# The old state set down by ScalarE, and small work moved to GpSimd, in an RWKV-7 and top-k expert kernel

## The chip, the cores and the metric

The kernel runs on one core of one Trainium2 chip. A core has TensorE (PE, matrix products), VectorE (DVE), ScalarE (ACT), GpSimd (POOL) and SyncE (SP, which here only issues transfers). The metric is the device time of one execution in microseconds, the median of several runs.

## The reference, cut to what matters

Two blocks follow each other. The first is a recurrence over 768 time steps for 4 batches of 8 heads, each with a state of 40 x 40:

```python
for t in range(S):
    y[:, :, t] = einsum('bhd,bhde->bhe', r_t, state)
    Sa = einsum('bhde,bhe->bhd', state, a_t)
    state = state * w_t[:, :, None, :] - einsum('bhd,bhe->bhde', Sa, b_t) + einsum('bhd,bhe->bhde', v_t, k_t)
```

The second takes the 3072 rows of `y` (320 wide) to one of 8 experts each. Of those that chose an expert, only the 80 with the largest gate weights are computed; all other rows are zero:

```python
expert_idx = argmax(x @ w_gate)
for e in range(E):
    tok_idx = the (at most) 80 rows of expert e with the largest gate_w
    out[tok_idx] = gate_w[tok_idx, None] * (maximum(x[tok_idx] @ w1[e], 0) @ w2[e])
```

## The kernel before, in words

**Units.** The recurrence is cut into chunks of 64 time steps; a unit is one chunk of a pair of batches (z) with all eight heads, so there are 24 units, and consecutive units belong to different pairs: a state written by unit n is read by unit n + 2. The heads stand in four pairs (g); the two heads of a pair (q) take the upper and lower 64 partitions. Within a chunk the decays are made cumulative (`pt` forwards, `qt` backwards, two DVE scans), the inputs are scaled with them, and the recurrence becomes products and the inversion of a unit-triangular matrix.

**Stages of a unit.** Seven units ahead, the preparation: `decays` (transpose w), `forward`, `backward`, `turned_a` and `decayed_a` (a, transposed, times `pt`), `doubled` (`qt` written twice side by side), `inverted` (transpose `qd`, multiply k and b: `scaled`), `operand`, `system` and `system_kept` (the matrix `nt`, sent to memory). Then the unit itself: `of_v`, `right` (adds the state times a), `diagonal`, `below`, `diagonal`, `beside`; `reads_g` transposes the state. One iteration later its output: `of_state`, `kept_state`, `turned`, `lower`, `summed`, then `logits`, and after one more iteration `logits_summed`.

**The output tile.** `y` is one PSUM tile (`ps_y` has one buffer), with 64 columns for outputs and 40 for the new state per head pair. `kept_state` puts the old state on those 40 columns by a product with the identity, four products a unit. `summed` adds the unit's contribution, then DVE multiplies the 40 columns by the last decay into `state` (line 522, one instruction for each q) and the other columns into `xT` (line 526). Until both are done, TensorE can't begin `of_state` of the next unit (line 416).

**The state.** It is kept with the two heads of a pair side by side, each on its own 64 partitions and zero on the other's, so that `right` can use it as the second operand of a product over 128 partitions.

**The inversion.** It is done on DVE for four units at a time, in 30 steps of two instructions (lines 381 and 384). `fetch` reads `nt` back from memory as `lt`, `begin` makes the start `tt` from it on GpSimd, `end` sends the solution to memory and reads it back as `dt`, which `diagonal` uses. In every group of four iterations, the first (n divisible by 4) fetches and begins, and the three others hold the steps: `pause(steps, us)` issues steps until their assumed cost is used up.

**Order.** Each engine works through its own queue in order, and `do` fixes that order as written in the loop over n: what stands earlier in the loop stands earlier in every engine's queue. A wait of one instruction holds all that is behind it on that engine. SyncE's queue of transfers is also in order.

**Selection and experts.** After the units, lists of the largest gate weights are merged, row numbers found by products with one-hot matrices, and the experts computed: `gather` (an indirect transfer by GpSimd), `tokens` (transpose), `first_half`, `second_half`, and an indirect transfer to the output. `keep_at_work` gives TensorE 40 products on a tile without meaning while the first rows are gathered. The small transfer `held` stands in SyncE's queue ahead of the weights of experts 3 to 7 and waits for the row numbers.

Of the kernel before, what the change touches and what calls it, by code (L numbers as in the profile page):

```python
# [8 lines left out]
F32 = mybir.dt.float32  # L9
BF16 = mybir.dt.bfloat16  # L10
I32 = mybir.dt.int32
AX = mybir.AxisListType.X
# [6 lines left out]
def kernel(  # L19
# [43 lines left out]
    NCI = NM // NG  # L63
    HB = 64
    assert N == B * S and DM == H * D and D <= HB and H % 2 == 0 and S % (2 * T) == 0 and BP == 2
    assert G * ZT == 512 and NG * 32 == 128 and E == 8 and 1 <= cap <= 128
    rounds = -(-cap // 8)
    capr = rounds * 8
    NF = DM // 128
# [60 lines left out]
    assert NL // NG >= 2 and capr <= 128 and NG * ZT <= MERGE + NG * capr  # L130


    ones_b = const.tile([128, 128], BF16, name="ones_b")
    behind_b = const.tile([128, 128], BF16, name="behind_b")
    seg_t = const.tile([128, E, 2 * NM], F32, name="seg")
    seg = seg_t.rearrange("p e m -> p (e m)")
    iot = const.tile([128, 1, cap], F32, name="iot")


    still = const.tile([128, 256], BF16, name="still")  # L140
    nc.vector.memset(still, 0.0)

    def keep_at_work(pool, tag, times, x=still):
        p = pool.tile([128, 256], F32, name="still_p", tag=tag)
        for _ in range(times):
            nc.tensor.matmul(p, lhsT=x[:, 0:128], rhs=x, start=True, stop=True)

    nc.gpsimd.tensor_copy(ones_b, ones)
    nc.gpsimd.tensor_tensor(out=behind_b, in0=strict, in1=ones, op=Alu.subtract)
    nc.gpsimd.memset(seg_t, 1.0)  # L150
    nc.gpsimd.memset(seg_t[:, :, 0:1], 0.0)
    iot_i = const.tile([128, cap], I32, name="iot_i")
    nc.gpsimd.iota(iot_i, pattern=[[1, cap]], base=1, channel_multiplier=0)
    nc.gpsimd.tensor_copy(iot[:, 0, :], iot_i)


    with ExitStack() as p1:
# [14 lines left out]
        def filled(name, n, shape, fill=0.0, where=lambda t: t):  # L172

            ts = [hold.tile(shape, F32, name=f"{name}{i}") for i in range(n)]
            for t in ts:
                engines[0].memset(where(t), fill)
                engines.reverse()
            return ts
# [13 lines left out]
        side = hold.tile([128, 1 + SLOTS, Z, H, HB], F32, name="side")  # L192
        nc.gpsimd.memset(side[:, 1:], 0.0)


        state = filled("state", BP, [128, Z * G * 2 * D + HB - D])
        og_t = filled("og", 2, [128, NG, 32])

        units = [(c, bp) for c in range(NC) for bp in range(BP)]
# [27 lines left out]
            return side[:, 1 + n % SLOTS]  # L227

        def own(n):
            return state[units[n][1]][:, 0 : Z * G * 2 * D].rearrange("p (z g q d) -> p z g q d", z=Z, g=G, q=2)  # L230

        def pairs(t):
            return t.rearrange("p (g q) d -> p g (q d)", q=2)
# [82 lines left out]

        def doubled(n):
            of[n]["qd"] = qd = sb.tile([128, G, Z, 2, T], F32, name="qd", tag="qd")
            nc.scalar.copy(qd.rearrange("p g z i t -> p (g z) i t"),  # L319
                           of[n].pop("qt")[:, :, :, 1:].rearrange("p g z t -> p (g z) t").unsqueeze(2)  # L320
                           .to_broadcast([128, G * Z, 2, T]))

# [105 lines left out]
        def kept_state(n):  # L428

            if n + BP < NU:  # L430
                for z in range(Z):
                    for q, m in enumerate(pars):
                        nc.tensor.matmul(of[n]["y"][m, z, :, T : T + D], lhsT=ident[m, m], rhs=own(n)[m, z, :, q, :],
                                         start=False, stop=False, skip_group_check=True)

        def right(n):
            o, sb_, pr = of[n], own(n), of[n]["pr"]
            for g in range(G):
                for z in range(Z):
                    nc.tensor.matmul(pr[halves[1 - z], 2 * g : 2 * g + 2, :], lhsT=o["ahT"][:, g, halves[z]],  # L440
                                     rhs=sb_[:, z, g, :, :], start=False, stop=False, skip_group_check=True)

        def right_kept(n):
            o = of[n]
# [25 lines left out]
                nc.scalar.copy(vu_of(n)[m, 1 - i, :, 0:D], of[n]["pr"][m])  # L470

        def reads_g(n):
            st = state[units[n][1]]
            p = ps_t.tile([128, Z, G, HB], F32, name="gp_", tag="t")
            for z in range(Z):
                for g in range(G):
                    for q, m in enumerate(pars):
                        at = ((z * G + g) * 2 + q) * D
                        nc.tensor.matmul(p[m, z, g, :], lhsT=st[m, at : at + HB], rhs=ident[m, m], start=z == 0 and g == 0,
                                         stop=True, skip_group_check=True)  # L480
            of[n]["gT"] = gT = sb.tile([128, Z, G, HB], F32, name="gT", tag="gT")
            nc.scalar.copy(gT, p)
# [25 lines left out]
        def summed(n):  # L508
            o = of[n]
            last = n + BP >= NU  # L510
            for z in range(Z):
                for g in range(G):
                    for q, m in enumerate(pars):
                        x = side[:, 0, z, 2 * g + q, :]
                        if not last:

                            x = bass.AP(x.tensor, x.offset, [x.ap[0], [(1 + n % SLOTS) * Z * H * HB, 2], [1, HB]])
                        nc.tensor.matmul(o["y"][m, z, g, 0 : T if last else T + HB], lhsT=o["s"][:, z, 2 * g + q, :], rhs=x,  # L518
                                         start=False, stop=True, skip_group_check=True)
            if not last:  # L520
                for q, m in enumerate(pars):
                    nc.vector.tensor_tensor(  # L522
                        out=own(n)[m, :, :, q, :], in0=o["y"][m, :, :, T : T + D],
                        in1=o["pt"][m, :, :, T : T + 1].rearrange("p g z o -> p z g o").to_broadcast([HB, Z, G, D]), op=Alu.mult)
            o["xT"] = xT = sb.tile([128, G, ZT], F32, name="xT", tag="xT")
            nc.vector.tensor_tensor(out=by_batch(xT).rearrange("p g z t -> p z g t"), in0=o["y"][:, :, :, 0:T],
                                    in1=o["pt"][:, :, :, 0:T].rearrange("p g z t -> p z g t"), op=Alu.mult)
            load(n + 3, "v")
# [20 lines left out]

        def logits_summed(n):  # L550
            i = share_of[n]
            nc.vector.tensor_reduce(logit[i][:, n - shares[i][0], :], of[n]["xb"][:, :, 2 * D :].rearrange("p g e -> p e g"),  # L552
                                    axis=AX, op=Alu.add)
            of[n].clear()

        def eight(src, dst, i, first=None):
# [110 lines left out]
        def do(f, *args):  # L667
            traced = nc.cur_bb.bb.instructions
            at = len(traced)
            f(*args)  # L670
            traced = nc.cur_bb.bb.instructions
            for i in traced[at:]:
                if i.engine in kinds:
                    if i.engine in latest:
                        tc.add_manual_dep(i, latest[i.engine], mybir.DependencyInfo(
                            mybir.DependencyClass.NoSync, mybir.DependencyReason.DATA), reason="order")
                    latest[i.engine] = i.name
# [4 lines left out]
        def pause(todo, us_):  # L682
            while todo and us_ > 0:
                cost, f = todo.pop(0)
                do(f)
                us_ -= cost
# [55 lines left out]
        for n in range(NU + 2):  # L742
# [29 lines left out]
                do(doubled, m + 1)  # L772
            if now:
                do(right_kept, n)
            if next_:
                do(turned_a, m + 1)
                do(decayed_a, m + 1)
            pause(small, 1)
            pause(steps, 0.7)
            if past:  # L780
                do(lower, o)
            if n == NU - 1:
# [13 lines left out]
            if not coming:  # L796
                pause(steps, 9 if n % NG == 1 else 5.5 if n % NG == 2 else 100)
                pause(rounds_, LISTS.get(n, 0))
            elif n % NG == 0:
                do(begin, m // NG)  # L800
            else:
                pause(steps, 6.7 if n % NG < NG - 1 else 100)
            if o >= 1:
                do(logits, o - 1)
            if turn:
# [25 lines left out]

    pieces = const.tile([128, NM, NP, E], BF16, name="pieces")
    rest = const.tile([128, NM, E], F32, name="rest")
    for x, last, first_piece in ((ids, 1, 0), (gates, 4, 2)):
        for i in range(first_piece, last):
            nc.gpsimd.tensor_copy(pieces[:, :, i, :], x)
            nc.gpsimd.tensor_tensor(out=rest if i + 1 < last else pieces[:, :, last, :], in0=x, in1=pieces[:, :, i, :], op=Alu.subtract)
            x = rest  # L840

    fw = ctx.enter_context(tc.tile_pool(name="fw", bufs=1))

# [19 lines left out]
    with ExitStack() as p2:  # L863
# [36 lines left out]
        for m0 in range(0, NM, CH):  # L900
# [3 lines left out]
            for m in range(m0, m0 + CH):  # L904
# [2 lines left out]
        late = const.tile([128, 256], BF16, name="late")  # L907
        nc.gpsimd.affine_select(out=late, in_=hot.rearrange("p m s -> p (m s)")[:, 0:256], compare_op=Alu.is_gt,
                                fill=0.0, base=-2, pattern=[[0, 256]], channel_multiplier=0)
        keep_at_work(ps_l, "still", 40, late)  # L910
        low = sl.tile([cap, NP * E], F32, name="low")
        nc.scalar.copy(low, ip)
        piece = [low[:, i * E : (i + 1) * E] for i in range(NP)]
# [65 lines left out]
    for e in range(4):  # L979
        gather(e)  # L980

    held = nc.dram_tensor("held", (cap, E), I32, kind="Internal")
    nc.sync.dma_start(held[:, :], idx_g)
    for e in range(3, E):
        weights_of(e)
    tokens(0)
# [34 lines left out]
```

## Time and profile before

| what | value |
|---|---|
| time, median of 3 (lowest to highest) | 620.43 us (619.39 to 623.21) |
| span of the profiled run | 618.5 us |
| busy: PE, DVE, ACT, POOL | 78%, 59%, 38%, 21% |
| granted TensorE clock, mean | 0.871 |
| preparation and first inversion | 0 to about 96 us |
| 24 units with their outputs | about 96 to 484 us |
| last selection | to about 517 us |
| eight experts | to 618.5 us |

Busy shares are means over stages with different limits, so what a change brings must be read in its own stage. The granted clock says at what part of full speed TensorE ran; it is 1.00 or 0.50 at any moment. A unit takes 14 to 19 us in the middle of the run; one (the sixth) took 23.

### The profile page before, as it was taken

To read this page: it belongs to the slowest core of one execution; us is meant where nothing else is said; L and a number is where in the kernel's file an instruction comes from. 1 tells how busy PE (TensorE), PEld (TensorE's weight loads), DVE (VectorE), ACT (ScalarE), POOL (GpSimd) and SP (SyncE) were. 2 spreads that over 40 slices of the span, in tenths; PEclk is the share of its full clock that TensorE was granted. 3 is DMA by queue.
4 is the path that set the end of the run, shared out by engine and by line. 5 is a ranking of instruction groups with operands and counts; after the bars stand their busy time and mean duration, and the time that the engine had idled before them with its cause. 6 is when DMAs were issued, how large, how long until landed. Compare 5 with 4: busy or idle time off the path is not lost. (4 is left out here: it accounts for less than half of the span.)

```text
span 618.5 us, 25228 instructions
## 1 busy us (share of the span) xinstructions
PE 480.6 (78%) x11281; PEld 411.2 (66%) x11281; DVE 362.5 (59%) x870; ACT 234.7 (38%) x418; POOL 130.2 (21%) x171
## 2 busy tenths in 40 slices
PE   2874039978979898978998898599888205999996
PEld 1653037867869787877887787488777204877874
DVE  8766932678547874888567853988266984001010
ACT  2462015645654655655564554154445000000000
POOL 5022003222221412422231133021112012111011
PEclk9986557989996989999998899799999556579999
DMA  4587077535777658765766345125210179995000
GB/s 75 109 165 134 11 122 124 95 64 116 137 122 145 133 128 153 144 140 96 141 113 121 73 87 103 33 70 79 49 33 14 21 258 347 330 334 158 14 14 14
DMA packets 236033, 71.46 MB, mean 116 GB/s; under 512 B 217236, under 2 KB 228756, under 8 KB 235924
## 3 DMA queue, kind: packets, MB, share of 16 engines
q1 hardware_dynamic: 223728, 66.47, 49.6%
q10 hardware_dynamic: 11428, 1.73, 1.7%
q8 instruction: 89, 1.46, 0.9%
q0 software_dynamic: 768, 1.64, 0.9%
q14 instruction: 20, 0.16, 0.1%
HBM read 51.69 MB, written 18.12 MB: 113 GB/s over the span
## 5 line engine op out<-in xcount | busy, mean ns | idle before, releaser
L272 POOL TENSOR_SCALAR_AFFINE_SELECT side<-side 64x1024 f32<-64x1024 f32 x47 | 55.3, 1176 | 113.0 <-ACT side L500 111.7
L384 DVE TENSOR_TENSOR tt<-tt,tmp 128x30 f32<-128x30 f32 (+9 forms) x180 | 71.2, 396 | 6.6
L381 DVE TENSOR_TENSOR tmp<-tt,lt 128x30 f32<-128x30 f32 (+9 forms) x180 | 65.2, 362 | 14.5 <-POOL tt L370 9.3
L272 POOL TENSOR_SCALAR_AFFINE_SELECT nt<-nt 64x512 f32<-64x512 f32 x48 | 34.4, 717 | 139.6 <-ACT nt L352 138.3
L416 PE MATMUL yp<-rT,gT 64*64 64x64 f32 x768 | 30.6, 231 | 35.9 <-DVE lg L552 28.2
L416 PEld LDWEIGHTS yp<-rT,gT 64*64 64x64 f32 x768 | 27.7, 145 | 37.8 <-issue 35.6
L319 ACT COPY qd<-qt 128x1024 f32<-128x1024 f32 x24 | 25.3, 1053 | 71.6 <-DVE qt L305 68.1
L974 DVE TENSOR_SCALAR y<-yp,weight 80x320 f32<-80x320 f32 x8 | 4.4, 548 | 79.4 <-PE yp L972 79.4
L522 DVE TENSOR_TENSOR state<-yp,pt 64x320 f32<-64x320 f32 x44 | 21.4, 487 | 50.1 <-PE yp L518 49.8
L518 PE MATMUL yp<-side,scaled 128*64 128x128 f32 (+1 forms) x768 | 47.5, 279 | 2.2 <-POOL side L272 2.2
L245 PE MATMUL tp<-ident,raw_a 128*128 128x128 f32 x96 | 19.2, 333 | 35.4 <-DMA raw_a<-in_a_dram 35.0
L518 PEld LDWEIGHTS yp<-side,scaled 128*64 128x64 f32 x768 | 41.9, 143 | 3.9 <-POOL side L272 2.4
L298 DVE TENSOR_TENSOR_SCAN pt<-decay,begins 128x520 f32<-128x520 f32 x24 | 30.3, 1263 | 20.2 <-ACT decay L292 20.0
L453 PE MATMUL pr<-yy,dt 32*32 32x40 f32 x1536 | 39.0, 203 | 3.7 <-ACT yy L446 1.8
L453 PEld LDWEIGHTS pr<-yy,dt 32*32 32x32 f32 x1536 | 32.6, 111 | 10.9 <-issue 5.7
L972 PE MATMUL yp<-w,hT 128*80 128x320 f32 x128 | 38.5, 448 | 0.0
L245 PEld LDWEIGHTS tp<-ident,raw_a 128*128 128x128 f32 x96 | 12.4, 166 | 38.5 <-issue 34.7
L966 ACT ACTIVATE hT<-hp 128x320 f32<-128x320 f32 x16 | 6.1, 434 | 83.3 <-PE hp L962 83.3
L955 PEld LDWEIGHTS hp<-xe,w 128*128 128x128 f32 x256 | 36.2, 227 | 1.5 <-issue 0.2
L955 PE MATMUL hp<-xe,w 128*128 128x80 f32 x256 | 36.4, 311 | 0.0
L266 PE MATMUL sp<-ahT,sT 64*64 64x64 f32 x1536 | 32.7, 241 | 2.3 <-ACT sT L342 2.3
L404 PE MATMUL pr<-side,nt 64*64 64x40 f32 x768 | 33.8, 235 | 0.4 <-issue 0.4
(300 smaller groups left out, 998.9 us busy)
## 6 DMA issues: line engine op xcount, KB each, us to landing
w<-in_moe_w_dram SPq DMA_DIRECT2D x8, 1280.0 KB, 14.1
w<-in_moe_w_dram SPq DMA_DIRECT2D x8, 1024.0 KB, 15.9
blocks<-nt SPq DMA_DIRECT2D x48, 128.0 KB, 2.5
raw_w<-in_w_dram SPq DMA_DIRECT2D x48, 80.0 KB, 3.2
raw_s<-in_b_dram SPq DMA_DIRECT2D x48, 80.0 KB, 2.9
raw_r<-in_r_dram SPq DMA_DIRECT2D x48, 80.0 KB, 3.1
side<-in_v_dram SPq DMA_DIRECT2D x48, 80.0 KB, 2.8
x_rows<-xb SPq DMA_DIRECT2D x48, 80.0 KB, 2.3
```

Source lines behind the costliest of these rows:

```text
L245: nc.tensor.transpose(p[:, g, :], t[:, g, :], ident)
L266: nc.tensor.matmul(p[i, q, z, g, :], lhsT=lhs[m, z, g, i], rhs=rhs[m, g, halves[z]], start=True, stop=True)
L272: nc.gpsimd.affine_select(out=o, in_=o, compare_op=Alu.is_gt, fill=0.0, base=0, pattern=[[0, o.shape[1]], [1, T]], channel_multiplier=-1)
L298: nc.vector.tensor_tensor_scan(flat(pt), flat(chunks(n)), flat(begins), 0.0, op0=Alu.mult, op1=Alu.add)
L381: nc.vector.tensor_tensor(out=tm, in0=t3[:, 0:i, i : i + 1].to_broadcast([128, i, n]), in1=l3[:, i : i + 1, i + 1 :].to_broadcast([128, i, ...
L384: nc.vector.tensor_tensor(out=t3[:, 0:i, i + 1 :], in0=t3[:, 0:i, i + 1 :], in1=tm, op=Alu.add)
L404: yield lambda h=h, z=z: nc.tensor.matmul(pr[halves[1 - z], h, :], lhsT=o["nt"][halves[z], z, of_head(n, h), :], rhs=vu[halves[z], z, h, 0:D],
L416: yield lambda z=z, g=g, m=m: nc.tensor.matmul(y[m, z, g, 0:T], lhsT=o["gT"][m, z, g, :], rhs=o["rT"][m, g, halves[z]], start=g == 0, stop ...
L453: nc.tensor.matmul(o["pr"][m, h, :], lhsT=dt_[m, (n % NG) * 2 * G + of_head(n, h), :], rhs=o["yy"][m, h, :], start=h == 0, stop=True, skip ...
L518: nc.tensor.matmul(o["y"][m, z, g, 0 : T if last else T + HB], lhsT=o["s"][:, z, 2 * g + q, :], rhs=x, start=False, stop=True, skip_group_ ...
L955: nc.tensor.matmul(hp[f // (FK // 2)][:, f % (FK // 2), :], lhsT=t1[:, i, f * 128 : (f + 1) * 128], rhs=xe[:, i, :], start=f % (FK // 2) = ...
L972: nc.tensor.matmul(yp, lhsT=hT[:, f, :], rhs=w2[:, f, :], start=f == 0, stop=f == FK - 1)
```

## The change

The old state is no longer put into `y` by four fp32 products with the identity. Two products of zeros in bf16 touch the 40 columns (so that later products add to what stands there), and ScalarE then copies the old state onto them (`state_kept`). The state becomes compact, without the zero halves, so that DVE writes it in one instruction; GpSimd copies it into one tile `apart` with the zero halves, which `right` reads. The doubling of the inverse decays goes from ScalarE to GpSimd, and the sum of the logits from DVE to GpSimd for the first 20 units. The inversion's steps are placed anew: some between `turned_a` and `decayed_a`, fewer later in the iteration. Constants that only the selection needs are made after the units. The filler products are 52 in place of 40, and `held` waits for the second gather in place of the row numbers.

```diff
         def own(n):
-            return state[units[n][1]][:, 0 : Z * G * 2 * D].rearrange("p (z g q d) -> p z g q d", z=Z, g=G, q=2)
+            return state[units[n][1]]
+
+        def own_apart(n):
+            for q, m in enumerate(pars):
+                nc.gpsimd.tensor_copy(apart[m, :, :, q, :], own(n)[m, :, :, 0:D].rearrange("p g z d -> p z g d"))
...
         def doubled(n):
...
-            nc.scalar.copy(qd.rearrange("p g z i t -> p (g z) i t"),
+            nc.gpsimd.tensor_copy(qd.rearrange("p g z i t -> p (g z) i t"),
...
                 for z in range(Z):
-                    for q, m in enumerate(pars):
-                        nc.tensor.matmul(of[n]["y"][m, z, :, T : T + D], lhsT=ident[m, m], rhs=own(n)[m, z, :, q, :],
-                                         start=False, stop=False, skip_group_check=True)
+                    nc.tensor.matmul(of[n]["y"][:, z, :, T : T + D], lhsT=still[:, 0:128],
+                                     rhs=still[:, 0 : G * D].rearrange("p (g d) -> p g d", g=G),
+                                     start=False, stop=False, skip_group_check=True)
+
+        def state_kept(n):
+            if n + BP < NU:
+                nc.scalar.copy(of[n]["y"][:, :, :, T : T + D], own(n)[:, :, :, 0:D].rearrange("p g z d -> p z g d"))
...
             if not last:
-                for q, m in enumerate(pars):
-                    nc.vector.tensor_tensor(
-                        out=own(n)[m, :, :, q, :], in0=o["y"][m, :, :, T : T + D],
...
+                nc.vector.tensor_tensor(
+                    out=own(n)[:, :, :, 0:D].rearrange("p g z d -> p z g d"), in0=o["y"][:, :, :, T : T + D],
...
+                if n + BP < NU:
+                    own_apart(n)
...
+            if n < NL:
+                part = sb.tile([128, G // 2, E], F32, name="part", tag="part")
+                nc.gpsimd.tensor_tensor(out=part, in0=x[:, 0 : G // 2], in1=x[:, G // 2 :], op=Alu.add)
+                nc.gpsimd.tensor_tensor(out=lg, in0=part[:, 0], in1=part[:, 1], op=Alu.add)
...
                 do(right_kept, n)
+            if past:
+                do(state_kept, o)
             if next_:
                 do(turned_a, m + 1)
+            pause(steps, 0.7)
+            if next_:
                 do(decayed_a, m + 1)
             pause(small, 1)
-            pause(steps, 0.7)
+            pause(steps, 0.4)
...
-                pause(steps, 6.7 if n % NG < NG - 1 else 100)
+                pause(steps, 5.5 if n % NG < NG - 1 else 100)
...
-        keep_at_work(ps_l, "still", 40, late)
+        keep_at_work(ps_l, "still", 52, late)
...
-    held = nc.dram_tensor("held", (cap, E), I32, kind="Internal")
-    nc.sync.dma_start(held[:, :], idx_g)
+    held = nc.dram_tensor("held", (cap, E), F32, kind="Internal")
+    nc.sync.dma_start(held[:, :], rows[1][:, 0:E])
```

## The prediction

> **What bounds the kernel now.** I read the page first, then the waits, then the timeline of the places where TensorE (PE) waits, with busy time by window.
>
> ```profile
> PE   2874039978979898978998898599888205999996
> PEclk9986557989996989999998899799999556579999
> ```
>
> One digit is 15.5 us. Slices 0 to 5 are the preparation and the first inversion (PE empty in slice 4), 6 to 30 the 24 units, 31 to 33 the selection, the rest the eight experts. In the units PE is 8 or 9 tenths busy: PE's own work and its waits set the time there. The clock falls after PE waits, and stays low at the start of the experts.
>
> ```profile
> PE tp L245 <- DMA raw_a<-in_a_dram: 35.0, 7, 27.5
> PE yp L416 <- DVE lg L552: 28.2, 12, 7.0
> POOL tt L370 <- DMA lt<-blocks: 54.1, 6, 11.7
> ```
>
> (total, times, longest.) 27.5 of the first line is the first inversion. The second is VectorE (DVE) arriving late at the end of a unit: it must write `state` and `xT` before `y` may be refilled. In steady units these waits are 2.1 to 3.0 us, after units 1 and 2 of each group of four, which carry the most inversion steps. The third costs nothing today: GpSimd (POOL) sits idle until `lt` arrives. It matters below.
>
> ```profile
> L433 PE MATMUL yp<-state,ident 64*64 64x160 f32 x176 | 19.3, 331 | 0.0
> L319 ACT COPY qd<-qt 128x1024 f32<-128x1024 f32 x24 | 25.3, 1053 | 71.6 <-DVE qt L305 68.1
> L522 DVE TENSOR_TENSOR state<-yp,pt 64x320 f32<-64x320 f32 x44 | 21.4, 487 | 50.1 <-PE yp L518 49.8
> ```
>
> These are what the change removes, halves or moves.
>
> ```profile
> 245.94 0.99 DVE L522 TENSOR_TENSOR state<-yp,pt 64x320 f32<-64x320 f32 x2 [5.73 <-PE yp L518]
> 249.62 0.77 PE L440 MATMUL pr<-state,ahT 128*64 128x80 f32 x16
> 249.83 1.76 POOL L370 TENSOR_SCALAR_AFFINE_SELECT tt<-lt 128x1024 f32<-128x1024 f32 x1 [9.56 <-DMA lt<-blocks]
> 251.47 0.63 PE L245 MATMUL tp<-ident,raw_a 128*128 128x128 f32 x4 [1.08 <-DMA raw_a<-in_a_dram]
> ```
>
> The passage from unit 8 to 9: PE reads the state at 249.62, before `tt` starts. In the same passage for units 4, 12 and 16, `tt` starts 3.0, 0.5 and 1.1 us after that read.
>
> ```profile
> 523.40:526.20 2.80, 0.00 (x0) 0.00 (x1) 0.00 (x0) 0.00 (x0) 0.72 (x1) 1.00 1.05 274
> 528.10:548.20 20.10, 20.10 (x102) 18.46 (x101) 0.41 (x1) 1.53 (x4) 0.91 (x1) 0.50 1.06 335
> ```
>
> Windows; second number its length, then PE busy, and near the end the clock. The 40 filler products end at 523.4, the first gathered rows come 2.8 us later, and then PE works without a gap for 20 us at half clock.
>
> [...]
>
> **Part by part.**
>
> *Old state.* Four fp32 products per unit (8 records) took 0.73 to 0.75 us at full clock (177.12 to 177.85). Two bf16 products with 160 columns replace them. A 128x256 bf16 filler took 0.083 us at full clock (12 in 1 us at 521 to 523), so two with their loads cost 0.15 to 0.3; I take 0.25. PE saves 0.48 per unit. ScalarE (ACT) gains a 128x320 copy, 0.43 by the 0.42 of `yy`. It is queued after `yy`, and behind it waits `side`, which cannot start before PE's scores, so it is free.
>
> *Doubling.* ACT loses 1.05 per unit. At 148.83 PE finished `right`, but `yy` waited for `qd` until 150.21 and PE's next product was held about 0.3: 0.25 saved. GpSimd's copy: 0.28 for 128 elements (L148) and 0.34 for 192 (L838) extrapolate to 1.1; the 128x1024 mask took 1.27; at the slope of its two-input rows (0.24 for 32 elements, 0.55 for 192) it would be 2.2. I take 1.15. [...] I charge 1.0 per group.
>
> *State compact.* One 128-partition multiply replaces two of 0.49: DVE saves 0.49 just before `xT`, where PE waits. `logits_summed` takes 0.20 off DVE after `xT`. Two 64x320 copies to `apart` come to GpSimd, 0.45 to 0.6 each (the 128x320 mask took 0.45); I take 1.0 together. In most units they end 1.1 after `state`, and `right` comes about 2 after it: hidden.
>
> *Steps.* Step 13 (0.80 with gaps 0.86) leaves unit 1's late part, and two or three steps go ahead of `ahT` and `scaled`, where DVE idles. Late waits 3.0 and 2.1 fall to about 0.5 each. But unit 3 inherits two more steps after `scaled` (128x168 and 128x150, 1.4 with gaps). `solved` and `dt` go out that much later, while PE arrives 0.75 earlier; `dt` was already just too late (PE paused 0.84 inside L453 at 238.32). New wait: about 2.2 in unit 0.
>
> *GpSimd's queue.* `begin` stands ahead of `apart` in unit 0. So `right` of unit 1 waits for `lt`, then `tt` 1.27, memset 0.15, copies 1.0: 2.5 with a hand-over. Unit 8 to 9: from the `dt` wait to `tt` 11.5, so copies done at 14.0; PE needs 11.3 less 0.5, 10.8. Stall 3.2 (3.7 by unit 12, 6.4 by unit 4); I take 3.5. It absorbs the `raw_a` wait of 1.1 to 1.4 behind it: net 2.3. Queued behind `right` is all of PE's unit.
>
> *Sum per group*: saved 1.9 + 1.0 + 4.1 = 7.0; added 2.2 + 2.3 + 1.0 = 5.5, plus 1.0 because longer waits keep the clock low longer (after the 3.26 wait at 178.5 it stayed at half for 13.7 us; after waits of 2 to 4 us for 3.4, in five of eight). Net -0.5; groups from units 5, 9, 13: -1.5. The first group has no stall behind `tt` in unit 1, and lost 3.9 and 2.2 to DVE: -4.5. At unit 17 DVE's own steps set the end: 0.
>
> *Units 18 to 23*: PE waits about 1.0 each for DVE, 11 busy of 12: -0.45 -0.48, six units: -5.5.
>
> *Start.* DVE's copies, begun at 5.37, were held until GpSimd's memsets ended at 9.08; six constants (1.7 us) leave that queue. Later the reload of `raw_s` sets the pace, and `qd` may cost a step or two: -1.5. The constants now run after 499.9 and are needed at 509.9: 0. SBUF pools: 0.
>
> *Experts.* Filler 12 x 0.083 = 1.0 longer, to about 524.4. `held` now waits for the second gather, so loads for experts 3 to 7 (issued at 518.25 before) no longer share the DMA engines with the first gathers; a scatter landed in 2.4 us, a gather in 6.4. Rows should come at 522 to 523.5: no gap. At full clock one expert takes 9.63 (561.28 to 570.91) and a first half 4.75; start plus 1.4 + 4.75 + 9.63 = 15.8, so expert 0 ends at 540.2 instead of 551.6. I take -11. Later loads start 4 to 6 us later; each lasts about 7.7 (2.6 MB at 340 GB/s), the last done near 565, needed near 580: 0.
>
> Total -1.5 -4.5 -1.5 -5.5 -11 = -24: 620.4 becomes 596.4, say 597.
>
> **Rivals.** (A) The stall behind `tt` grows and keeps PE at half clock each time, like unit 5 (23.3 us against 18.5): +6 a group, 615. For: the 6.4 of unit 4. Against: clocks stayed full from 220 to 333 through waits of 3.0. (B) The experts stay cold: only 2 us gained there, 606. For: 1 to 2 us of gaps remain around the first rows. Against: waits of 1.0 to 1.4 never halved it. [...] (D) The stall is hidden (SyncE reaches `lt` earlier): 586.
>
> **Numbers.** Main 0.50, A 0.15, B 0.17, C 0.12, D 0.06. Range 582 to 618 leaves out C and half of what lies below D. Faster by over 1% (below 614.2): main, D, B, a fifth of A: 0.76; within 1%: 0.14; slower: 0.10.
>
> **What would show it.** PE's L416 waits on DVE below 10 us in total; PE waiting on the `apart` copies three or four times, 3 to 4 us each; `dt` pauses of 2 us in units 4, 8, 12; clock 1.00 from the first expert, its scatter near 11 us earlier in the tail. Wrong if the clock at the experts is 0.50, if L416 waits persist, or if GpSimd's `qd` takes near 2 us.

## The result, and the profile after

The changed kernel takes 600.15 us (median of 4 runs, 597.08 to 601.77), where the kernel before took 621.42 (4 runs, 619.39 to 623.21): a ratio of 0.9653, 95% interval 0.9600 to 0.9705. On a second chip it took 600.62 against 620.99, 0.9723 (0.9631 to 0.9814). The forecast was 597, range 582 to 618. Ratios, here and below, leave out executions that were over 1.5% slower than the fastest of the same kernel.

The two profiled runs (spans 618.5 and 597.7 us) are cut here at the start of `right` of certain units and at the first product of the last selection (`thr_p`):

| stretch | before | after | difference | forecast |
|---|---|---|---|---|
| start to `right` of unit 0 | 96.57 | 96.05 | -0.5 | -1.5 |
| units 0 to 4 | 66.50 | 60.21 | -6.3 | -4.5 |
| units 4 to 16 | 204.06 | 202.19 | -1.9 | -1.5 |
| units 16 to 18 | 32.69 | 34.49 | +1.8 | 0 |
| units 18 to 23 | 63.27 | 60.79 | -2.5 | -5.5 |
| unit 23 to `thr_p` | 45.63 | 45.54 | -0.1 | 0 |
| `thr_p` to the end (experts) | 109.78 | 98.43 | -11.35 | -11 |

More than half of the gain lies in the last sixth of the run. Not all lines of the table are equally firm. Three more profiled runs of the old units (experiments 1 to 3) and four of the changed ones show how far chance goes: units 0 to 4 took 61.2 to 66.5 us before and 60.2 to 62.3 after, units 4 to 16 took 200.7 to 204.1 and 199.9 to 202.7. The rise at units 16 to 18 (32.4 to 33.8 before, 34.3 to 36.2 after) and the gain at 18 to 23 (62.8 to 63.8, then 60.1 to 61.4) stand clear of it.

The page of the changed kernel, busy tenths and granted clock in 40 slices:

```profile
PE   4775028899879988689879998789998502999996
PEclk9977559889989999799998997979998755899999
```

One slice is 14.9 us. After the selection (slices 32 and 33, counted from 0) the clock is at 8 in the first slice of the experts and at 9 in the next; before, slices 34 and 35, with PE at 9, stood at 5 and 7 (the page of the kernel before is in the prediction). Windows of the changed kernel from just before the first gathered rows show it directly (length, PE busy, and near the end the clock):

```profile
514.90:520.00 5.10, 5.00 (x47) 4.30 (x45) 0.81 (x2) 0.00 (x0) 1.81 (x2) 1.00 0.62 181
520.00:540.00 20.00, 20.00 (x154) 15.72 (x154) 0.86 (x2) 2.29 (x6) 1.86 (x2) 1.00 1.05 346
```

In the units the account is less simple. First the wait of the kernel before at the refill of `y` that adds to the 28.2 us on `lg` in the prediction, then TensorE's waits in the changed kernel (total, times, longest):

```profile
PE yp L416 <- DVE xT L526: 7.0, 3, 3.9
```

```profile
PE pr L434 <- POOL apart L219: 14.4, 4, 6.5
PE pp L320 <- POOL qd L308: 13.3, 14, 1.6
PE yp L405 <- DVE xT L519: 10.3, 11, 4.3
PE pr L447 <- DMA dt<-solved: 3.5, 4, 1.7
PE yp L405 <- DVE lg L551: 2.0, 1, 2.0
```

The 35.2 us of waits on DVE at the refill of `y` (28.2 and 7.0 before) are 12.3 now. Two waits on GpSimd that did not exist before, 14.4 and 13.3, have come in; 6.8 of the 13.3 lie in the preparation, so 20.9 of the two fall into the units. From `right` of unit 0 to `right` of unit 23, in one window, the kernel before and then the changed one (length, PE busy):

```profile
96.57:463.09 366.52, 320.67 (x9370) 283.83 (x9367) 248.53 (x592) 189.17 (x340) 88.50 (x101) 0.94 0.54 104
```

```profile
96.05:453.73 357.68, 312.01 (x9238) 275.98 (x9235) 252.15 (x550) 181.25 (x346) 146.26 (x201) 0.94 0.55 107
```

The stretch is 8.8 us shorter; TensorE's busy time fell by 8.7, its idle time stayed at 45.8 and 45.7. The fifth busy number is GpSimd's: 88.5 to 146.3. So in this pair of runs the waits only changed hands, and what was won is time in which TensorE worked. How much was won is less sure. The same old units in the profile of experiment 2:

```profile
98.10:460.46 362.36, 311.56 (x9369) 275.13 (x9366) 249.32 (x592) 189.02 (x340) 88.44 (x101) 0.97 0.55 105
```

The four profiles of the old units are 362.4 to 366.5 us long, with TensorE busy for 311.6 to 320.7 and idle for 45.9 to 50.8; five of the changed units are 357.7 to 359.9 long, 310.4 to 314.9 busy and 45.0 to 47.5 idle. The gain of the units is therefore between 2.5 and 9 us, and the two ranges of idle time overlap. The busy time goes with the clock too (320.7 at a mean clock of 0.94, 311.6 at 0.97): it stood at 0.50 for 19 to 45 us of the old units and for 34 to 51 us of the changed ones. Groups of the changed kernel (count, total busy us, mean ns of one, idle time before):

```profile
L421 PE MATMUL yp<-still 128*128 128x160 bf16 x44 | 7.0, 242 | 1.1 <-issue 1.1
L513 DVE TENSOR_TENSOR state<-yp,pt 128x320 f32<-128x320 f32 x22 | 10.7, 488 | 49.7 <-PE yp L510 49.7
L308 POOL COPY qd<-qt 128x1024 f32<-128x1024 f32 x24 | 25.1, 1046 | 33.2 <-DVE qt L294 31.8
```

The products of zeros are busy 7.0 us where the identity products were 19.3; the state write is as long for 128 partitions (488 ns) as it was for 64 (487) and is done half as often; `qd` costs GpSimd what it cost ScalarE (1053). All three durations came close to the forecast. The wait at `right` of unit 9, in the timeline (start, length):

```profile
234.72 0.49 DVE L513 TENSOR_TENSOR state<-yp,pt 128x320 f32<-128x320 f32 x1 [5.80 <-PE yp L510]
...
242.22 1.26 POOL L359 TENSOR_SCALAR_AFFINE_SELECT tt<-lt 128x1024 f32<-128x1024 f32 x1 [12.70 <-DMA lt<-blocks]
...
243.60 0.95 POOL L219 COPY apart<-state 64x320 f32<-64x320 f32 x2
...
244.61 1.33 PE L434 MATMUL pr<-apart,ahT 128*64 128x80 f32 x16 [6.51 <-POOL apart L219]
```

The state is written at 235.2 and its two copies last 0.95, but they are queued behind `tt`, and `tt` waits for a transfer. Now the wait for `qd`, in one unit of the changed kernel:

```profile
190.97 1.36 DVE L287 TENSOR_TENSOR_SCAN pt<-decay,begins 128x520 f32<-128x520 f32 x1
191.32 1.02 POOL L548 TENSOR_TENSOR part<-xb 128x16 f32<-128x16 f32 x1
...
192.68 1.45 DVE L294 TENSOR_TENSOR_SCAN qt<-decay,ends 128x520 f32<-128x520 f32 x1
192.99 2.35 POOL L261 TENSOR_SCALAR_AFFINE_SELECT nt<-nt 64x512 f32<-64x512 f32 x2
...
195.41 1.08 POOL L308 COPY qd<-qt 128x1024 f32<-128x1024 f32 x1
...
196.54 0.72 PE L320 MATMUL pp<-ident,qd 64*128 64x64 f32 x16 [1.08 <-POOL qd L308]
```

`qt` was ready at 194.13. `qd` starts at 195.41, when the mask of `nt` ahead of it in GpSimd's queue is done, and GpSimd had no pause since 190.30. Two things made that queue long. The small sum `part` took 1.02 us beside a DVE scan; it did so in ten units of this run, and 0.21 to 0.26 in the ten where no scan ran beside it (0.22 at 404.67). And the first of the two masks took 1.59 us beside the second scan, the second mask 0.70.

### The profile page after: what moved, and what is told of

Read it like the earlier page. It is cut to its first block, busy times and chain, and to the rows that moved or that the text cites. A ratio compares the mean times of both kernels' runs of the same rounds, so it can differ in the third digit from the quotient of the medians.

```text
span 597.7 us, 25130 instructions
## 1 busy us (share of the span) xinstructions
PE 463.8 (78%) x11161; PEld 397.0 (66%) x11161; DVE 368.2 (62%) x829; ACT 218.9 (37%) x416; POOL 196.2 (33%) x279
## 3 DMA queue, kind: packets, MB, share of 16 engines
q1 hardware_dynamic: 223728, 66.47, 50.8%
## 5 line engine op out<-in xcount | busy, mean ns | idle before, releaser
L370 DVE TENSOR_TENSOR tmp<-tt,lt 128x30 f32<-128x30 f32 (+9 forms) x180 | 73.0, 406 | 19.4 <-POOL tt L359 14.6
L373 DVE TENSOR_TENSOR tt<-tt,tmp 128x30 f32<-128x30 f32 (+9 forms) x180 | 76.9, 427 | 6.6
L219 POOL COPY apart<-state 64x320 f32<-64x320 f32 x44 | 19.8, 450 | 109.3 <-DVE state L513 102.0
L261 POOL TENSOR_SCALAR_AFFINE_SELECT nt<-nt 64x512 f32<-64x512 f32 x48 | 40.7, 849 | 35.5 <-ACT nt L341 29.7
L513 DVE TENSOR_TENSOR state<-yp,pt 128x320 f32<-128x320 f32 x22 | 10.7, 488 | 49.7 <-PE yp L510 49.7
L405 PE MATMUL yp<-rT,gT 64*64 64x64 f32 x768 | 28.4, 224 | 12.3 <-DVE xT L519 10.3
L331 ACT COPY sT<-tp 128x512 f32<-128x512 f32 x48 | 25.8, 591 | 32.5 <-PE tp L243 32.1
L308 POOL COPY qd<-qt 128x1024 f32<-128x1024 f32 x24 | 25.1, 1046 | 33.2 <-DVE qt L294 31.8
L255 PE MATMUL sp<-rT,vuT 64*64 64x64 f32 x1536 | 32.6, 241 | 3.1 <-ACT nt L341 2.3
L294 DVE TENSOR_TENSOR_SCAN qt<-decay,ends 128x520 f32<-128x520 f32 x24 | 32.6, 1359 | 2.8 <-DVE ends L292 0.5
L320 PE MATMUL pp<-ident,qd 64*128 64x64 f32 x384 | 21.8, 261 | 15.4 <-POOL qd L308 13.3
```

The costliest lines, as they stand in the source:

```text
L255: nc.tensor.matmul(p[i, q, z, g, :], lhsT=lhs[m, z, g, i], rhs=rhs[m, g, halves[z]], start=True, stop=True)
L261: nc.gpsimd.affine_select(out=o, in_=o, compare_op=Alu.is_gt, fill=0.0, base=0, pattern=[[0, o.shape[1]], [1, T]], channel_multiplier=-1)
L294: nc.vector.tensor_tensor_scan(flat(qt)[:, ::-1], decay[n % 2][:, 1:][:, ::-1], flat(ends)[:, ::-1], 0.0, op0=Alu.mult, op1=Alu.add)
L308: nc.gpsimd.tensor_copy(qd.rearrange("p g z i t -> p (g z) i t"), of[n].pop("qt")[:, :, :, 1:].rearrange("p g z t -> p (g z) t").unsqueeze ...
L331: nc.scalar.copy(sT[:, :, :, m], p)
L370: nc.vector.tensor_tensor(out=tm, in0=t3[:, 0:i, i : i + 1].to_broadcast([128, i, n]), in1=l3[:, i : i + 1, i + 1 :].to_broadcast([128, i, ...
```

## The experiments

All times are medians with the lowest and highest run in brackets; ratios are to the kernel before on the same chip; stretches are of the profiled run. "Units" is `right` of unit 0 to `right` of unit 23, "experts" `thr_p` to the end, as above. Five profiled runs of the changed kernel's units (in five kernels that differ only at the experts) gave 357.68, 358.02, 357.87, 357.75 and 359.87, so about 2 us there can be chance; four of the old units (the kernel before and experiments 1 to 3) gave 366.52, 362.40, 362.36 and 362.83, so there it is about 4.

**1 to 3. The edits at the experts, alone and together, on the kernel before.**

```diff
-    held = nc.dram_tensor("held", (cap, E), I32, kind="Internal")
-    nc.sync.dma_start(held[:, :], idx_g)
+    held = nc.dram_tensor("held", (cap, E), F32, kind="Internal")
+    nc.sync.dma_start(held[:, :], rows[1][:, 0:E])
```

That is the first (`tail_held`); the second (`tail_fill`) has `keep_at_work(ps_l, "still", 52, late)` instead; the third (`tail_both`) has both.

> The kernel before, with one edit: the small transfer ahead of the weights of experts 3 to 7 waits for the second gather; 40 fillers as before. Theory (an uncontended gather closes the gap): rows of expert 0 are there when the fillers end, the clock at the first expert is 1.00, and the time is 610 (-11). Rival (the length of the filler run is what keeps the clock): a gap stays, the clock falls to 0.50, and the time is 618 to 621.

> The kernel before, with one edit: 52 fillers in place of 40. Theory (the gather is what matters): the fillers end about 1.0 later, the rows still land 9 us after the fillers began, 1 to 2 us of gap stay, and the time is 619 to 621. Rival (the fillers keep the clock): gap too short to halve the clock, 610.

> The kernel before, with both edits at the experts and nothing else. Theory: -11, so 610, which leaves 10 of the 21 us to the recurrence. Rival: the early part also brings the experts into a better phase of the clock, and the edits alone bring under 6, 615 or more.

The fillers alone: 621.52 (613.77 to 626.35, 20 runs), ratio 0.9983 (0.9952 to 1.0013), no change. `held` alone: 606.83, 611.90, 623.80, 623.94. Both: 606.58, 611.24, 620.74, 621.08. So the later loads bring 10 us or more, but only in every second run of the old units; no run of the other half was profiled. The profile of the fillers alone, timeline and then windows:

```profile
514.70 8.36 PE L146 MATMUL still_p<-late 128*128 128x256 bf16 x52
...
523.70 0.33 PE L942 MATMUL xp<-ident,rows 80*128 80x80 f32 x2 [0.64 <-DMA rows<-x_rows,idx_g]
...
525.46 0.36 PE L942 MATMUL xp<-ident,rows 80*128 80x80 f32 x2 [1.15 <-DMA rows<-x_rows,idx_g]
```

```profile
519.90:526.70 6.80, 5.01 (x47) 4.03 (x45) 0.82 (x2) 0.00 (x0) 2.90 (x4) 1.00 1.07 315
526.70:547.10 20.40, 20.40 (x100) 18.00 (x99) 0.00 (x0) 1.53 (x4) 0.60 (x1) 0.50 1.06 325
```

With the fillers the clock comes to 1.00, there are two gaps of 0.64 and 1.15 us, and then TensorE works 20.4 us at half clock. With `held` late the rows came 7.9 and 8.1 us after the first filler, against 9.0 here and 9.3 in the kernel before, and the profiled runs stayed at 1.00.

**4. `begin` one iteration later**, so that the copies to `apart` stand ahead of it in GpSimd's queue.

```diff
+            if n % NG == 1 and m - 1 < NU:
+                do(begin, (m - 1) // NG)
...
-            elif n % NG == 0:
-                do(begin, m // NG)
-            else:
+            elif n % NG:
```

> The changed kernel, but the start of the inversion on GpSimd stands one iteration later, behind the mask of nt and the doubling, so that the copies of the state no longer stand behind a wait for a transfer. Theory (the stall of TensorE behind that wait costs 3.5 to 6.5 us in units 5, 9 and 13): TensorE's waits on the copies fall from 14.4 in total to under 1, the inversion starts 1 to 2 us later, and the time falls by 6 to 10, to 591 to 594. Rival (the arrival of the transfer sets the pace of a group anyway): the wait only moves, to dt or to DVE, and the time stays within 2 us of 600.

Measured 609.90 (603.11 to 612.97), ratio 0.9767 (0.9693 to 0.9841); units 358.75. Its waits:

```profile
PE tp L234 <- DMA raw_a<-in_a_dram: 34.9, 4, 28.2
PE yp L405 <- DVE xT L519: 12.5, 9, 6.2
...
PE pr L447 <- DMA dt<-solved: 8.1, 6, 2.6
```

The 14.4 us on `apart` are gone, and the units are no shorter. TensorE's wait on `raw_a` is 6.7 us beyond the first inversion's 28.2 (0.5 in the changed kernel), on `dt` 8.1 (3.5), and on DVE's `xT` 2.2 more. The wait only moves, as the rival said. The profiled run is longer than the changed kernel's because its experts began at half clock (108.41), not because of the units.

**5 to 8, on one chip.** The changed kernel again, and with one part undone each. First the changed kernel as it is, and with the old tail (`held` and 40 fillers as before). The windows that some expectations speak of can be seen in the profiles of the kernel before and of the changed one: every stretch of the granted clock at 1.00 or at 0.50, but for the last, which the end of the run cuts off, is a multiple of 3.41 us long (3.41 to 112.6 us, then 3.41 to 85.3).

> The changed kernel as it is, on the chip of the runs beside it, so that its loop can be compared by stage. Expected by both theories: 597 to 602 us, right of unit 0 near 96, right of unit 23 near 453.7, thr_p near 499.3, experts at clock 1.00 from 515. If the clock of the experts is a matter of where the throttle's windows fall, one of its runs may come out near 611.

> The changed kernel with the old tail: held depends on the indices again and 40 fillers. Theory 1 (the 20.8 us are two separate parts: about 9.5 in preparation and units, 11.35 in the experts): right of unit 23 near 453.7 as in the changed kernel, experts begin at half clock for about 20 us, 611 us in all. Theory 2 (a loop with fewer waits leaves the throttle in a state that keeps the experts fast, the tail's edits are beside the point): 599 to 602. Theory 3 (the loop gained nothing, the difference is of the tail alone): 620.

Again: 600.62 (599.48 to 606.93), units 358.02, experts 98.52. With the old tail: 612.64 (611.23 to 613.12), ratio 0.9890 (0.9827 to 0.9954), units 357.87, experts 109.73. So the units and what goes with them are worth 8.4 us (620.99 to 612.64; by the interval of the ratio 3 to 11) and the tail 12.0 (to 600.62): the first theory. The timeline with the old tail shows the gaps that the old tail leaves:

```profile
516.36 0.33 PE L957 MATMUL xp<-ident,rows 80*128 80x80 f32 x2 [1.82 <-DMA rows<-x_rows,idx_g]
...
518.33 0.36 PE L957 MATMUL xp<-ident,rows 80*128 80x80 f32 x2 [1.35 <-DMA rows<-x_rows,idx_g]
```

Then the doubling back on ScalarE:

```diff
-            nc.gpsimd.tensor_copy(qd.rearrange("p g z i t -> p (g z) i t"),
+            nc.scalar.copy(qd.rearrange("p g z i t -> p (g z) i t"),
```

> The changed kernel with only the doubling put back on ScalarE. In the changed kernel TensorE waited 13.3 us in 14 places for the doubling on GpSimd. [...] Theory 2 (a trade: yy and side now stand behind qd on ScalarE, and TensorE's waits come back as shorter waits on ScalarE; the chain of transfers sets the groups of four anyway): the stretch is within 2 us of the changed kernel's. Theory 3 (it was a gain, as predicted 1.0 per unit of four): 2 to 4 us longer.

The median is 600.47, but the runs spread over 594.78, 595.34, 600.47, 606.21 and 609.99; units 355.62. The waits on GpSimd's `qd` are gone, and the groups show what came back (idle time before the line, by what ended it); on `yy` TensorE did not wait here in the changed kernel:

```profile
L447 PE MATMUL pr<-yy,dt 32*32 32x40 f32 x1536 | 39.8, 204 | 10.3 <-ACT yy L440 6.2 <-DMA dt<-solved 3.2 <-issue 0.5
L320 PE MATMUL pp<-ident,qd 64*128 64x64 f32 x384 | 21.8, 250 | 6.2 <-ACT sT L331 2.0 <-ACT decay L281 1.7 <-ACT qd L308 1.5
```

A trade, close to the second theory, with about 2 us in favour of ScalarE (355.62, where the changed kernel beside it has 358.02). The third falls. The scans stayed at 1.31 and 1.37 us (1.37 and 1.33 in the run beside it), though GpSimd no longer doubled; it isn't `qd` that makes them longer than the 1.26 and 1.24 of the kernel before. The profiled run had a gap of 0.55 us before the first rows and its experts at half clock (106.92), which hides those 2 us in its total.

Last the old state as four identity products:

```diff
-                    nc.tensor.matmul(of[n]["y"][:, z, :, T : T + D], lhsT=still[:, 0:128],
-                                     rhs=still[:, 0 : G * D].rearrange("p (g d) -> p g d", g=G),
-                                     start=False, stop=False, skip_group_check=True)
+                    for q, m in enumerate(pars):
+                        nc.tensor.matmul(of[n]["y"][m, z, :, T : T + D], lhsT=ident[m, m], rhs=own(n)[m, :, z, 0:D],
+                                         start=False, stop=False, skip_group_check=True)
...
-            if past:
-                do(state_kept, o)
```

> The changed kernel with only the old state brought into y by four fp32 identity products again, not by two products of zeros and a copy by ScalarE. Theory 1 (TensorE's own work sets the pace of the units): about 0.44 us more per unit in 22 units, so right of unit 0 to right of unit 23 plus 6 to 9 us, and 606 to 609 in all. Theory 2 (in the groups of four the chain of transfers and GpSimd's queue sets the pace): less than 3 us more, most of it in units 18 to 21, and the waits on apart and dt shorter by what the products take.

The four runs took 600.45, 606.45, 609.97 and 621.34, median 608.21. The profiled one is the slowest of them; its units took 367.62:

```profile
97.77:465.39 367.62, 326.48 (x9370) 288.53 (x9367) 250.68 (x550) 173.97 (x324) 150.07 (x201) 0.93 0.54 104
```

TensorE's busy time is 15.4 us up on the run beside it (311.03), its idle time 5.9 down. `apart` waits fell from 14.9 to 5.1, but `dt` waits rose from 3.3 to 9.9. That would be the first theory: TensorE's own work sets the pace, in the groups of four as well. But it rests on the slowest run, in which the clock was at 0.50 for 52 us of the units (41 in the run beside it) and the experts too began at half clock (108.16). The products themselves were busy for 17.4 us in it, 10.4 more than the products of zeros. The fastest run contradicts it: with the shortest start, selection and experts of all profiles (96.0, 45.3 and 97.4), an estimate, this run (its span was 598.7) leaves at most 360 for the units, where the theory asks for 364 or more. The runs of the changed kernel beside it, 599.48 to 606.93, overlap with these. So what the identity products cost in the time is not shown.

**9 to 12, on a third chip.** What keeps the experts warm (at full clock), and what the placing of the steps is worth. The changed kernel with 68 and with 40 fillers, and 68 with the doubling on ScalarE:

```diff
-        keep_at_work(ps_l, "still", 52, late)
+        keep_at_work(ps_l, "still", 68, late)
```

> The changed kernel with 68 filler products in place of 52. So far the first gathered rows came 7.9 to 9.0 us after the fillers began, and 52 of them last 7.2 to 8.4: with 16 more at 0.083 us each TensorE has no gap. Theory 1 (a gap between the fillers and the first rows is what sends the experts to half clock): every run warm, 598 to 602, the experts at 1.00 from the first, at most 1 us lost to fillers that run longer than needed. Theory 2 (the gap is not it; where the throttle's windows fall decides): some runs near 598 and some near 610.

> The changed kernel with the doubling back on ScalarE and 68 fillers. With the doubling alone put back, two runs took 595, one 600.5 and two 606 to 610, and the profiled one had a gap of 0.55 us before the first rows and experts at half clock, with a stretch of units 2.1 to 2.4 us shorter. Theory 1 (closing the gap keeps the experts warm): all runs 594 to 598, below the changed kernel with 68 fillers by 2 to 3. Theory 2 (windows decide): spread 595 to 610 as before.

> The changed kernel with 40 fillers, held still behind the second gather. It tells the 12 fillers from the held loads in the changed kernel. Theory 1 (a gap cools the experts): 40 fillers end 1 us earlier, the rows come 1.0 to 1.8 us after them, and most runs are near 610, as when both are undone (612.6). Theory 2 (the early rows alone do it): 598 to 602 in every run.

68: 601.68 (599.99 to 602.21), experts 99.07. 68 with ScalarE: 599.88 (598.37 to 602.91), units 353.82, experts 99.58. 40: 601.27 (600.72 to 602.23), experts 97.44. All twelve runs lie between 598.37 and 602.91: none shows the 10 us of cold experts. With 68 the gap is closed, as the first theory wants; but with 40 there is a gap and it does no harm, against it:

```profile
511.25 6.55 PE L139 MATMUL still_p<-late 128*128 128x256 bf16 x40
...
518.38 0.33 PE L957 MATMUL xp<-ident,rows 80*128 80x80 f32 x2 [0.57 <-DMA rows<-x_rows,idx_g]
```

So more fillers brought nothing that can be seen (0.4 us between the medians of 68 and 40; 52 did not run on this chip), and the later loads did the work: the kernel with 40 fillers differs from the one of experiment 6 (612.64, on another chip) in them alone. The doubling on ScalarE with warm experts has the lowest median of this chip, 1.8 us below the same fillers with GpSimd, but the ranges overlap; its units are again shorter than those of all five runs of the changed kernel's.

Then the steps of the inversion where they were before:

```diff
-            pause(steps, 0.7)
-            if next_:
                 do(decayed_a, m + 1)
             pause(small, 1)
-            pause(steps, 0.4)
+            pause(steps, 0.7)
...
-                pause(steps, 5.5 if n % NG < NG - 1 else 100)
+                pause(steps, 6.7 if n % NG < NG - 1 else 100)
```

> The changed kernel with the steps of the inversion where the kernel before had them (a share of 0.7 of the step behind the decays, 6.7 after the second wait). Theory 1 (the placing took the waits on VectorE away): waits of TensorE for the end of a unit come back to 2 to 3 us in two units of four, the stretch from right of unit 0 to right of unit 23 is 5 to 8 us longer than the changed kernel's 357.8, most of it in units 0 to 4, 605 to 608 in all. Theory 2 (the halved state write and the moved sum did it): within 2 us of the changed kernel's stretch, waits on VectorE at 10 to 14 us in all. Either way the profile's stretch decides, not the total, which also holds the clock of the experts.

The four runs took 603.69, 604.08, 610.97 and 613.30, median 607.52, all above the twelve runs beside them (602.91 at most). The profiled run is the one of 610.97: units 368.19, experts 98.92. Window and waits:

```profile
96.04:464.23 368.19, 315.06 (x9238) 278.76 (x9235) 246.10 (x550) 181.07 (x346) 147.19 (x201) 0.94 0.54 104
```

```profile
PE yp L405 <- DVE xT L519: 19.1, 13, 3.1
PE pp L320 <- POOL qd L308: 15.3, 14, 2.1
```

DVE waits went from 10.3 to 19.1 (1.2 to 2.4 us in two units of each later group) and TensorE's idle time from 45.7 to 53.1: the first theory. The 10 us of the profiled run came mostly after unit 4 (units 0 to 4 only 3 longer), which it had wrong. Two of the runs were 7 us faster than the profiled one, so the placing is worth somewhere between about 2 and 10 us.

## Why the prediction was right, and where its sum was not

The time holds, and so does the tail: worth 11 (measured 11.35, and 12.0 when undone). In the units the forecast events came, DVE's late waits going and a wait behind `tt` coming, but their sum was too large: 11.5 us forecast, 8.8 measured in the profiled pair and 2.5 to 9 over all profiles. In the pair the misses partly cancel: units 0 to 4 gained 1.8 more than forecast, units 16 to 23 4.8 less.

- **Experts.** Right in size and in its main cause, the loads kept away from the first gathers. The second cause, longer fillers, wasn't one: alone 0.9983, and 40 do as well as 68. The forecast "no gap" came true (0.10 us). Against rival B the prediction said that waits of 1.0 to 1.4 never halved the clock; in four of the variants half clock followed gaps of 0.55 to 1.15 us, and in the kernel before the clock fell at 101.0, 1.8 us after a wait of 1.34. It gave rival B, experts that stay cold, 0.17; the chance is real in the variants: begun with a gap of 0.55 to 1.02 us, four profiled runs were cold.
- **DVE.** "Late waits 3.0 and 2.1 fall to about 0.5 each" held: 0.56, 0.68 and smaller. The placing of the steps did most of that: with the steps in their old place the late waits of the groups from unit 5 on are 1.2 to 2.4 us each again (2.1 to 3.0 in the kernel before).
- **GpSimd's queue.** "I take 3.5" for each of three groups was 3.62, 6.51 and 3.50 in this run and 5.83, 4.03 and 4.43 in the next: the mechanism right, the size about 1 us low. The `raw_a` waits behind it were absorbed, as said. Rival D, with the stall hidden and 586, did not come; and taking the stall away by starting the inversion later (experiment 4) made the units no shorter.
- **Doubling: the step that failed.** Among the waits that the prediction names there is none behind `qd`. The copy's length was right (1.05 us for the 1.15 taken), its place in the queue wasn't looked at: `part` and the mask of `nt` stand ahead of it, and both took longer beside a scan (1.02 for 0.22, 1.59 for 0.70). 13.3 us of waits in 14 places followed, five of them in the preparation (0.74 to 1.61 us, 6.8 in all). Undoing the move makes the units 2 to 4 us shorter (355.62 and 353.83). It isn't why the start gained only 0.5 of the forecast 1.5: with the doubling on ScalarE the start took 96.34 and 97.63, no less. The 1.0 us that the sum adds per group for the doubling was the author's estimate, and no run shows it. What the changed kernel shows, beside the waits on `qd`, is six steps of the inversion that took 1.05 to 1.12 us beside the copy, where the shortest of the same shapes took 0.21 to 0.40 (a 128x30 step 1.08 at 110.86 and 0.21 elsewhere).
- **Units 18 to 23.** Forecast -5.5, measured -2.5. The waits fell by 2.9 (6.9 to 4.0), as forecast. But the old state is set down only where n + 2 < 24, in four of the six units, and its saving was 1.7 us of busy time (3.06 to 1.32), not 2.9; the stretch has five periods, not six; and 2.1 us came back at TensorE without a wait that the profile names: pauses that it calls "issue", for which it shows no cause (0.3 to 1.0 in the stretch, as 0.21 at 408.25 in the middle of `diagonal`), and products that are busy longer, such as the scores of line 255 (6.2 to 6.9). The clock was at 0.50 for 2.9 us of the stretch, 1.8 before.
- **Unit 17.** Forecast 0, measured +1.8. In the other four runs of the changed kernel's units this stretch takes 34.3 to 36.2, in the four of the old units 32.4 to 33.8, and with the steps in their old place 32.52: the placing that gains elsewhere seems to cost about 2 here.

DVE and GpSimd each took longer beside the other. In the kernel before, a 128x130 step on DVE took 1.25 us at 152.92, while GpSimd masked `side` until 154.04, and 0.29 at 119.22; in the changed kernel GpSimd's `part` went from 0.22 to 1.02 us beside a scan. The prediction also says that the clock falls after TensorE's waits. It doesn't after each: in the kernel before, waits of 2.10, 2.23 and 2.81 us were each followed by half clock (at 350.2, 217.1 and 333.1), three others of 2.07 to 3.00 were not.

Open: why a gap cools the experts in one run and not in another. Of fourteen profiled runs, five had no gap (0.1 us) and all stayed at 1.00; two had over 1.8 us and both fell to 0.50; of seven with 0.55 to 1.27, three stayed (0.57, 0.91, 1.27) and four fell (0.55, 0.64, 0.94, 1.02). The three runs with the old loads (the kernel before, `tail_fill`, `loop_only`) had a second gap of 0.50 to 1.35 us at the next rows, and all three fell; with the later loads that second gap is missing, so it can be part of what the loads cost, but three runs fell without it. In the kernel before, in `tail_fill` and in `qd_scalar` the clock fell 6.8 us after it had come back, for 17 to 20.5 us of work without a gap. Where in those 6.8 us the gap lies doesn't tell them apart either. Also open: what the products of zeros, the compact state and the sum on GpSimd are each worth in the units, and `qd` on ScalarE together with `part` back on DVE, which would take both off GpSimd's queue; neither was run.

## What to carry to other kernels

When an operation moves to an idler engine, its duration is the small question: look at what stands ahead of it in that engine's queue at the moment it is needed, and at what that in turn waits for. If waits only change hands, they win little: TensorE's idle time in the units was 45.9 to 50.8 us before and 45.0 to 47.5 after, while 22.9 us of waits on DVE had gone. Before a gain is put down to a stage, profile the kernel before more than once: its units differed by 4 us from run to run. And a transfer that isn't urgent should be kept away from the one that ends an idle time: the tail was worth 12 us here, because without it the experts fell to half clock for some 20 us.

## What the runs showed of the hardware

- Zero products followed by a ScalarE copy onto the same PSUM columns, with later products adding to them, work as a way to bring in an old value: 0.31 us a unit on TensorE instead of 0.75, and 0.44 on ScalarE.
- An elementwise product on DVE over 128 partitions (320 elements each) takes as long (488 ns) as over 64 (487).
- A two-input GpSimd operation of 16 elements takes 0.22 us alone and 1.02 beside a scan of 1.36 us on DVE (ten of twenty in one run); a 64 x 512 mask there takes 0.66 alone and about 1.5 beside a scan.
- Where TensorE waited for the first gathered rows, they came 7.1 to 8.6 us after the first filler when the weight loads waited, 8.4 to 9.3 when they didn't. From its first rows to its last product the first expert takes 15.3 us at full clock and 23.3 to 26.3 when the clock falls.
